# Running products of decays in chunked attention: two scans in place of a tree of products

## The chip, the cores and the metric

The kernel runs on one core of one Trainium2 chip. The metric is the device time of one execution in microseconds (us). Time is told in the profile's names: PE is TensorE (matmuls; PEld its weight loads), DVE is VectorE, ACT is ScalarE, POOL is GpSimd, SP the queue that issues DMAs.

## The reference, cut to what matters

A linear attention with decays, then a mixture of eight experts whose gate weights are balanced by eight Sinkhorn steps, then a wide layer with `h * cos(h)`. Only the attention is touched by the change:

```python
# q, k, v, alpha: (4, 8, 768, 48), alpha in 0.8 .. 1.0
for t in range(S):
    state = alpha[:, :, t, :, None] * state + einsum('bhd,bhe->bhde', k[:, :, t], v[:, :, t])
    y[:, :, t] = einsum('bhd,bhde->bhe', q[:, :, t], state)
x = y as (3072 tokens, 384)
logits = x @ w_gate; P = exp(logits - max); 8 x (rows to sum 1, columns to sum 1, times N/E)
out = sum over e of P[:, e] * (relu(x @ w1[e]) @ w2[e])        # 384 -> 1024 -> 384
h = out @ w_in; result = (h * cos(h)) @ w_out                  # 384 -> 2048 -> 384
```

## The kernel before, in words

**Two stages.** `stage1` interleaves the attention with the first expert's pass; `stage2` runs the other seven experts and the last layer in blocks of 512 tokens. Weights and activations are split into a rounded part and a rest, so that a product takes three matmuls in a fast format.

**Attention.** Tokens are worked in 12 units of 256 (`UNITS`), heads in four pairs, so there are 48 slots (`slots`). A slot's `q`, `k` and decays come in one tile `t` of three rows of 256 (a ring of four tiles, three of which lie in `acc`, whose end is free until the last units' expert products). In a slot the tokens form four chunks of 64, and every chunk two halves of 32. The chunked form needs `q` times the product of decays from the half's start up to its own token, `k` times the product of decays after its token to the half's end, and each half's whole product.

**`ew(i)`** prepares slot `i` with elementwise work. DVE clamps the decays into `a` (`dec`). POOL multiplies `q` by `a`. Then a tree over five levels follows: at level `l` DVE multiplies neighbouring products of decays (128, 64, 32, 16, 8 elements, kept in `pr` at offsets `po[l]`), and half of `q` and half of `k` (256 elements in one view) are multiplied by the products of the level before, at the first level by POOL, at levels 2 to 5 by DVE. One more product of four elements gives the chunks' whole decay, `pr` at `po[6]`. Three products then make `X` (second halves of `q`, once for either head) and `k6` (first halves of `k`), ACT copies the other halves, a reciprocal `rp` of the halves' products is taken, and POOL multiplies parts of `q` and `k` by it in place.

**The main loop** per slot: PE transposes `k6` into bank 0 (`pt`), ACT copies it; PE makes the scores `pg` in bank 1 from `t`; DVE copies them under a mask into `X` (two masked copies); PE makes `k`-`v` products `pk` in bank 2, DVE steps the state four times (`step`); a slot later PE makes the outputs `py` in bank 3, and ACT copies them to `x`. POOL also takes the clamped decays from the given ones and ACT squares and sums the difference into `adev`: if a decay was outside the range, a general path runs instead. `ew(i + 2)` is recorded ahead of slot `i`'s main part.

**What sets the order.** Nothing is issued as it is written: `Plan` records every instruction with its operands, and `issue` then replays a model of the engines with assumed costs (`_cost`) and latencies (`LAT`). It always gives the next instruction to the engine that can start first, by rank (0 first): 0 the attention's main part and Sinkhorn, 1 the experts' matmuls, 2 `ew`, 3 the check of the decays and the decode of the last layer's weights. The device then runs each engine's queue in that fixed order. All planned instructions have one line in the profile (L167), the line that issues them.

**Around it.** A unit's expert block takes its `x`, 8 hidden tiles of 18 matmuls each with 256 columns (banks 4 to 7), ReLU by ACT, and the rest of the rounded hidden layer by DVE (`act_relu`). The gate logits of the units feed `sinkhorn`, which starts when all of them are there; its result goes to DRAM (`pt`) and comes back spread over the partitions (48 transfers). Then the other experts follow.

Of the kernel before, what the change touches and what calls it, by code (L numbers as in the profile page):

```python
# [9 lines left out]
F32 = mybir.dt.float32  # L10
# [5 lines left out]
ALU = mybir.AluOpType  # L16
# [7 lines left out]
E = 8  # L24
# [14 lines left out]
FARENA, RARENA = 9204, 10240  # L39
# [21 lines left out]
class Plan:  # L61
    """Records engine instructions in program order, then issues them in the order in which a model of the
    engines would start them: what feeds the tensor engine first, its own attention products before the experts'."""

    # from one engine's end to another's start, with room for what the model misses
# [44 lines left out]
    def _cost(self, eng, name, aps, kw):  # L110
# [67 lines left out]
class Arena:  # L178
    """Tiles cut out of a buffer, which another stage cuts in another way."""
# [16 lines left out]
    def ring(self, n, shape, dtype):  # L196
        return ring([self.tile(shape, dtype) for i in range(n)])


def ring(tiles):  # L200
    """Tiles that take turns."""
    tiles = itertools.cycle(tiles)
    return lambda: next(tiles)


class Weights:
    """The passes' weights in chunks of 256 hidden units, as rounded parts and their rests."""
# [14 lines left out]
    def prep(self):  # L222
        """Split the next half of a chunk and load another one."""
# [12 lines left out]
class Passes:  # L236
    """Expert passes: hidden layer of a block, then its product with the second weight, LAG tiles behind."""
# [21 lines left out]
    def second(self):  # L259
# [39 lines left out]
class Kernel:  # L299
# [27 lines left out]
    # ------------------------------------------------------------ shared pieces  # L327
# [15 lines left out]
    def gate_weights(self, w):  # L343
        """Gate weights' rounded parts in columns 0..7 and rests in 8..15 of a full stationary tile."""
# [21 lines left out]
    def pieces(self, yt, t0, n):  # L366
        """The last pair's heads, 16 rows to each of the three row tiles."""
# [4 lines left out]
    # ------------------------------------------------------------ attention, chunks of 64  # L372
    def attention(self, pool):
# [6 lines left out]
        prs, k6s = (pool.ring(3, [128, UN], F32) for _ in range(2))  # L380
        rps, kts = pool.ring(3, [128, UN // 32], F32), pool.ring(2, [128, nt0, D], F32)
        yts = pool.ring(1, [128, UN], F32)
        adev, m1, m2 = (pool.tile([128, c], F32) for c in (NPAIR * len(UNITS), 1, 1))
        m2 = m2[0:1]
# [3 lines left out]
        dec, mask = ring([z.tile([128, UN], F32) for z in late]), self.mask  # L388
# [21 lines left out]
        def ew(i):  # L410
            t = loaded.pop(i)
            n = UNITS[slots[i][0]][2]
            X, pr, k6, rp, a = xt(), prs(), k6s(), rps(), dec()
            self.rank(2)
            po, o = {}, 0
            for l in range(1, 7):
                po[l] = o
                o += n >> l
            state[i] = dict(X=X, pr=pr, po=po, k6=k6, qk=t, a=a)
# [16 lines left out]
            tt(V, vw(pr, po[6], [[1, nb]]), vw(pr, po[5], [[2, nb]]), vw(pr, po[5] + 1, [[2, nb]]))  # L436
            for p0, h in ((0, 1), (64, 0)):
                p1 = p0 + 64
                tt(V, vw(X, h * UN + 32, [[64, nb], [1, 32]], p0, p1), vw(t, 32, [[64, nb], [1, 32]], p0, p1), vw(pr, po[5], [[2, nb], [0, 32]], p0, p1))
                A.copy(vw(X, h * UN, [[64, nb], [1, 32]], p0, p1), vw(t, 0, [[64, nb], [1, 32]], p0, p1))  # L440
            tt(V, vw(k6, 0, [[64, nb], [1, 32]]), vw(t, UN, [[64, nb], [1, 32]]), vw(pr, po[5] + 1, [[2, nb], [0, 32]]))
            A.copy(vw(k6, 32, [[64, nb], [1, 32]]), vw(t, UN + 32, [[64, nb], [1, 32]]))
            V.reciprocal(rp[:, :n // 32], vw(pr, po[5], [[1, n // 32]]))
# [17 lines left out]
        V.memset(adev, 0.0)  # L461
        V.tensor_copy(mask, mf)
# [402 lines left out]
```

## Time and profile before

| what | value |
|---|---|
| runs, median of 3 | 2338.79 us (2337.37 to 2341.6) |
| profiled execution, span | 2336.7 us |
| PE busy | 2268.1 us, 97% |
| DVE busy | 1091.0 us, 47% |
| POOL busy | 825.4 us, 35% |
| ACT busy | 782.3 us, 33% |
| chain that ended last | PE 85%, DVE 11% |

The profile gives the span of its execution, from the first to the last instruction, and no other time of it. Times are us, means of one instruction are in ns. [...] A matmul's record can include waiting, so a busy PE is not PE at its peak. The row of a group gives its busy time, the mean of one and the idle time of the engine ahead of it.

### The profile page before, as it was taken

The numbers are of one execution on the slowest core, as the hardware profiler recorded it, in microseconds if no ns is written. First come the engines' busy times: TensorE is split into PE (matmuls) and PEld (weight loads), VectorE is DVE, ScalarE is ACT, GpSimd is POOL, SyncE is SP. The second block draws the span as 40 slices with busy tenths as digits, with TensorE's granted clock in tenths as the row PEclk, the third lists the DMA queues.
The fourth block names the chain that finished last, engine by engine and source line by source line (L and its number), as shares of the span: only waits on it lengthen the run. The fifth ranks groups of instructions, "written<-read, shape, count | busy, mean of one in ns | idle before, by whom it ended". The sixth has DMA issues, their size and how long they took to land.

```text
span 2336.7 us, 32693 instructions
## 1 busy us (share of the span) xinstructions
PE 2268.1 (97%) x12790; PEld 1896.4 (81%) x12790; DVE 1091.0 (47%) x2417; ACT 782.3 (33%) x1628; POOL 825.4 (35%) x716
## 2 busy tenths in 40 slices
PE   4999999988999999999999999999999999999998
PEld 3878888976888888888888888888888888999997
DVE  8989988888422122212221222122222227767665
ACT  3444444221122113112211211211221136666664
POOL 6444443132234115213321422322242245457442
PEclk9988999999999999999999999999999999999999
DMA  4222222344111002001100200110020010000000
GB/s 149 65 66 73 71 73 58 99 119 129 49 30 43 5 10 64 9 6 37 36 7 8 63 10 5 43 30 10 5 63 10 5 43 13 1 8 28 27 28 29
DMA packets 70709, 94.93 MB, mean 41 GB/s; under 512 B 6992, under 2 KB 52624, under 8 KB 70544
## 3 DMA queue, kind: packets, MB, share of 16 engines
q1 hardware_dynamic: 70544, 92.74, 13.8%
q8 instruction: 102, 1.67, 0.3%
q14 instruction: 63, 0.52, 0.1%
HBM read 80.42 MB, written 11.11 MB: 39 GB/s over the span
## 4 chain that ended last, share of the span: by engine, by line
PE 85%; DVE 11%; DMA 1%; issue 1%; POOL 1%; ACT 0%; SPq 0%; DVEq 0%; POOLq 0%; ACTq 0%
PE bank L167 85%; DVE fbuf L167 8%; DVE acc L167 2%; DMA fbuf<-pt 1%; DVE rbuf L167 1%; POOL acc L167 0%; DVE P L167 0%; ACT fbuf L167 0%; POOL fbuf L167 0%; DMA pt<-fbuf 0%; DMA fbuf<-in_w_dram 0%; DMA w<-fbuf 0%; SPq L167 0%; ACT rbuf L167 0%; POOL w31l L167 0%
## 5 line engine op out<-in xcount | busy, mean ns | idle before, releaser
L167 DVE SCALAR_TENSOR_TENSOR rbuf<-bank,rbuf 128x512 fp32r<-128x512 f32 (+1 forms) x432 | 271.8, 629 | 899.8 <-ACT rbuf L167 898.8
L167 ACT ACTIVATE rbuf<-bank 128x512 fp32r<-128x512 f32 (+1 forms) x432 | 237.1, 549 | 964.3 <-PE bank L167 954.5
L167 POOL TENSOR_TENSOR rbuf<-x,rbuf 128x512 fp32r<-128x512 f32 (+1 forms) x162 | 189.6, 1196 | 774.7 <-ACT rbuf L167 738.8
L167 POOL TENSOR_TENSOR acc<-acc,fbuf 128x512 f32<-128x512 f32 (+1 forms) x162 | 183.7, 1161 | 241.1 <-DVE fbuf L167 197.2
L167 PE MATMUL bank<-rbuf,w01h 128*128 128x512 f32 (+1 forms) x648 | 209.2, 379 | 1.3 <-DVE fbuf L167 1.3
L167 PE MATMUL bank<-rbuf,w21h 128*128 128x512 f32 (+1 forms) x648 | 205.7, 374 | 3.5 <-DVE rbuf L167 3.5
L167 PE MATMUL bank<-rbuf,w31h 128*128 128x512 f32 (+1 forms) x648 | 206.5, 376 | 1.9 <-DVE rbuf L167 1.9
L167 PE MATMUL bank<-rbuf,w11h 128*128 128x512 f32 (+1 forms) x648 | 205.2, 374 | 2.2 <-DVE rbuf L167 2.2
L167 POOL TENSOR_TENSOR rbuf<-fbuf,rbuf 128x512 fp32r<-128x512 f32 x96 | 129.0, 1345 | 191.1 <-ACT rbuf L167 190.3
L167 PE MATMUL bank<-rbuf,w20h 128*128 128x512 f32 (+1 forms) x792 | 193.0, 378 | 2.3 <-DVE rbuf L167 2.3
L167 PE MATMUL bank<-rbuf,w00h 128*128 128x512 f32 (+1 forms) x792 | 194.0, 378 | 0.9 <-ACT rbuf L167 0.9
L167 PE MATMUL bank<-rbuf,w10h 128*128 128x512 f32 (+1 forms) x792 | 194.6, 381 | 0.0
L167 PE MATMUL bank<-rbuf,w30h 128*128 128x512 f32 (+1 forms) x792 | 192.8, 378 | 0.0
L167 PEld LDWEIGHTS bank<-rbuf,w20h 128*128 128x128 f32 x792 | 141.8, 190 | 30.0 <-DVE rbuf L167 2.5
L167 PEld LDWEIGHTS bank<-rbuf,w10h 128*128 128x128 f32 x792 | 143.3, 193 | 27.8
L167 PEld LDWEIGHTS bank<-rbuf,w00h 128*128 128x128 f32 x792 | 142.3, 190 | 28.9 <-ACT rbuf L167 1.2
L167 DVE SCALAR_TENSOR_TENSOR fbuf<-fbuf 128x192 uint32<-128x192 uint32 (+2 forms) x288 | 162.5, 565 | 6.1
L167 PEld LDWEIGHTS bank<-rbuf,w30h 128*128 128x128 f32 x792 | 141.9, 190 | 27.8
L167 DVE TENSOR_TENSOR fbuf<-bank,fbuf 128x512 f32<-128x512 f32 x126 | 82.9, 685 | 142.5 <-PE bank L167 138.8
L167 ACT ACTIVATE fbuf<-fbuf 128x512 f32<-128x512 f32 (+1 forms) x204 | 135.0, 662 | 42.4 <-DVE fbuf L167 40.8
L167 DVE TENSOR_SCALAR fbuf<-fbuf 128x192 uint32<-128x192 uint32 (+3 forms) x240 | 102.0, 441 | 99.9 <-ACT fbuf L167 93.5
L167 PEld LDWEIGHTS bank<-rbuf,w01h 128*128 128x128 f32 x648 | 122.4, 194 | 25.9 <-DVE fbuf L167 1.8
(117 smaller groups left out, 4111.5 us busy)
## 6 DMA issues: line engine op xcount, KB each, us to landing
raw<-in_wts_dram SPq DMA_DIRECT2D x64, 384.0 KB, 3.1
acc<-in_qka_dram SPq DMA_DIRECT2D x36, 384.0 KB, 3.2
fbuf<-in_w_dram SPq DMA_DIRECT2D x64, 192.0 KB, 2.4
fbuf<-pt SPq DMA_DIRECT2D x48, 256.0 KB, 4.9
w<-fbuf SPq DMA_DIRECT2D x64, 96.0 KB, 2.4
raw<-w SPq DMA_DIRECT2D x16, 384.0 KB, 3.0
fbuf<-in_vv_dram SPq DMA_DIRECT2D x24, 192.0 KB, 3.2
fbuf<-in_qka_dram SPq DMA_DIRECT2D x12, 384.0 KB, 3.1
```

The costliest lines, as they stand in the source:

```text
L167: getattr(getattr(self.nc, eng), name)(*args, **kw)
```

## The change

In `ew`, the tree is replaced by two scans. A scan goes along a row and keeps `state = data0 * state + data1` at every element. The decays are clamped into a tile `a` of 8 segments of 33 elements, whose first element is zero, and `heads` is one at every segment's first element and zero elsewhere. So each segment restarts at one and then holds the running products of its 32 decays. `f` is the forward scan, `bwd` the same from the end to the start, with views of negative stride. `q` is multiplied by `f` (POOL) and `k` by `bwd` (DVE), each in one product of 256 elements. A half's whole product is the last element of its segment in `f`; `tot` is the product of a chunk's two. POOL's subtraction for the check of the decays moves from the main loop (rank 3) into `ew` (rank 2).

The tiles: `decs` and `fwds` are rings of two of 265 and 264 elements, `bwd` and `heads` are single, `tot` is a ring of three; `k6s` moves into the end of `acc`, where `dec` was. The arena is 28 elements larger; `lt` and `wgs` in `stage1` share a place. `Plan` learns a cost for the scan and the extent of views with negative stride. Comments go too.

```diff
+SEG = 32
+SCAN = (SEG + 1) * (UN // SEG)
...
+        if name == "tensor_tensor_scan":
+            return 67 + 2.1 * n
...
-            V.tensor_scalar(a[:, :n], t[:, 2, :n], AMIN, AMAX, op0=ALU.max, op1=ALU.min)
-            tt(G, t[:, 0, :n], t[:, 0, :n], a[:, :n])
-            tt(V, vw(pr, po[1], [[1, n // 2]]), vw(a, 0, [[2, n // 2]]), vw(a, 1, [[2, n // 2]]))
-            a1 = vw(t, 1, [[UN - 1, 2], [2, n // 2]])
-            tt(G, a1, a1, vw(a, 0, [[1, 2], [2, n // 2]]))
-            for l in range(2, 6):
-                h = 1 << (l - 1)
-                nb = n // (2 * h)
-                tt(V, vw(pr, po[l], [[1, nb]]), vw(pr, po[l - 1], [[2, nb]]), vw(pr, po[l - 1] + 1, [[2, nb]]))
-                a1 = vw(t, h, [[UN - h, 2], [2 * h, nb], [1, h]])
-                tt(V, a1, a1, vw(pr, po[l - 1], [[1, 2], [2, nb], [0, h]]))
-            nb = n // 64
-            tt(V, vw(pr, po[6], [[1, nb]]), vw(pr, po[5], [[2, nb]]), vw(pr, po[5] + 1, [[2, nb]]))
+            V.tensor_scalar(vw(a, 1, seg), vw(t, 2 * UN, flat), AMIN, AMAX, op0=ALU.max, op1=ALU.min)
+
+            V.tensor_tensor_scan(out=f[:, :SCAN], data0=a[:, :SCAN], data1=self.heads, initial=0.0, op0=ALU.mult, op1=ALU.add)
+            V.tensor_tensor_scan(out=vw(bwd, SCAN, [[-1, SCAN]]), data0=vw(a, SCAN, [[-1, SCAN]]), data1=self.heads, initial=0.0, op0=ALU.mult, op1=ALU.add)
+            tt(G, vw(t, 0, flat), vw(t, 0, flat), vw(f, 1, seg))
+            tt(V, vw(t, UN, flat), vw(t, UN, flat), vw(bwd, 2, seg))
+            G.tensor_tensor(out=vw(t, 2 * UN, flat), in0=vw(t, 2 * UN, flat), in1=vw(a, 1, seg), op=ALU.subtract)
+            first, second = SEG, 2 * SEG + 1
+            tt(V, tot[:, :nb], vw(f, first, [[2 * SEG + 2, nb]]), vw(f, second, [[2 * SEG + 2, nb]]))
...
-                G.tensor_tensor(out=d, in0=d, in1=st["a"][:, :n], op=ALU.subtract)
```

**DVE, in the middle of the attention, the work of about one slot.** `bank_97` is a hidden tile of the expert; `fbuf` and `acc` hold the attention's tiles. Before:

```order
L167 TENSOR_TENSOR acc<-acc,fbuf 128x2x16x8
L167 TENSOR_TENSOR fbuf<-acc 128x128
L167 TENSOR_TENSOR acc<-acc,fbuf 128x2x8x16
L167 SCALAR_TENSOR_TENSOR rbuf<-bank_97,rbuf 128x256
L167 TENSOR_TENSOR fbuf<-acc,fbuf 64x4x32 x2
L167 TENSOR_TENSOR fbuf<-acc,fbuf 128x4x32
L167 TENSOR_TENSOR fbuf<-fbuf 128x64
L167 TENSOR_TENSOR fbuf<-fbuf 128x32
L167 TENSOR_TENSOR fbuf<-fbuf 128x16
L167 TENSOR_TENSOR fbuf<-fbuf 128x8
L167 TENSOR_TENSOR fbuf<-fbuf 128x4
L167 RECIPROCAL fbuf<-fbuf 128x8
```
Now (a scan prints as SCALAR_TENSOR_TENSOR of 128x264):

```order
L173 SCALAR_TENSOR_TENSOR rbuf<-bank_97,rbuf 128x256
L173 TENSOR_SCALAR fbuf<-acc 128x8x32
L173 TENSOR_TENSOR fbuf<-acc,fbuf 64x4x32 x2
L173 SCALAR_TENSOR_TENSOR fbuf<-fbuf 128x264
L173 SCALAR_TENSOR_TENSOR fbuf<-fbuf,bank_95 128x48
L173 SCALAR_TENSOR_TENSOR fbuf<-fbuf 128x264
L173 SCALAR_TENSOR_TENSOR fbuf<-fbuf,bank_95 128x48
L173 COPY_PREDICATED fbuf<-mask,bank_94 64x256
L173 SCALAR_TENSOR_TENSOR fbuf<-fbuf,bank_95 128x48
L173 COPY_PREDICATED fbuf<-mask,bank_94 64x256
L173 TENSOR_TENSOR acc<-acc,fbuf 128x256
L173 RECIPROCAL fbuf<-fbuf 128x8
```
The products of 64 to 8 elements and all but one of those of 256 are gone; two scans stand in their place, with the state steps (128x48 from `bank_95`) and masked copies between them.

**POOL, in the attention.** `128x256` on `acc` is a product by decays or the subtraction, `128x2x128` the first level's product, `128x2x4x32` that by `rp`, `rbuf<-x` the rest of an expert's input. Before:

```order
L167 TENSOR_TENSOR acc<-acc,fbuf 128x2x4x32
L167 TENSOR_TENSOR rbuf<-x,rbuf 128x256
L167 TENSOR_TENSOR acc<-acc 128x256
L167 TENSOR_TENSOR acc<-acc,fbuf 128x2x4x32
L167 TENSOR_TENSOR acc<-acc 128x2x128
L167 TENSOR_TENSOR fbuf<-fbuf,acc 128x256
L167 TENSOR_TENSOR acc<-acc 128x256
L167 TENSOR_TENSOR rbuf<-x,rbuf 128x256
L167 TENSOR_TENSOR fbuf<-fbuf,acc 128x2x128
```
Now:

```order
L173 TENSOR_TENSOR acc<-acc,fbuf 128x256 x3
L173 TENSOR_TENSOR acc<-acc,fbuf 128x2x4x32
L173 TENSOR_TENSOR rbuf<-x,rbuf 128x256 x3
L173 TENSOR_TENSOR acc<-acc,fbuf 128x256 x3
L173 TENSOR_TENSOR acc<-acc,fbuf 128x2x4x32
L173 TENSOR_TENSOR fbuf<-fbuf 128x256 x2
L173 TENSOR_TENSOR acc<-acc,fbuf 128x2x4x32
L173 TENSOR_TENSOR acc<-acc,fbuf 128x256 x2
L173 TENSOR_TENSOR fbuf<-fbuf 128x2x4x32
L173 TENSOR_TENSOR acc<-acc,fbuf 128x256
```
The first level's products are gone, and the product by `f` and the subtraction, which both read the slot's scan tiles in `fbuf`, stand together ahead of the product by `rp`.

**PE, the rows up to the expert's first matmul.** `bank_93` holds the transposed `k6`, `bank_94` the scores, `bank_95` the `k`-`v` products, `bank_96` the outputs. Before:

```order
L167 MATMUL bank_93<-ident,fbuf 64x48 x8
L167 MATMUL bank_94<-acc 64x64 x8
L167 MATMUL bank_95<-fbuf 48x48 x8
L167 MATMUL bank_93<-ident,fbuf 64x48 x12
L167 MATMUL bank_94<-acc 64x64 x8
L167 MATMUL bank_96<-fbuf 48x64 x8
L167 MATMUL bank_95<-fbuf 48x48 x8
L167 MATMUL bank_93<-ident,fbuf 64x48 x4
L167 MATMUL bank_94<-acc 64x64 x8
L167 MATMUL bank_96<-fbuf 48x64 x8
L167 MATMUL bank_95<-fbuf 48x48 x8
L167 MATMUL bank_97<-rbuf,w00h 128x256
```
Now:

```order
L173 MATMUL bank_93<-ident,acc 64x48 x8
L173 MATMUL bank_94<-acc 64x64 x9
L173 MATMUL bank_96<-fbuf 48x64 x7
L173 MATMUL bank_95<-fbuf 48x48 x8
L173 MATMUL bank_96<-fbuf 48x64
L173 MATMUL bank_93<-ident,acc 64x48 x8
L173 MATMUL bank_94<-acc 64x64 x8
L173 MATMUL bank_93<-ident,acc 64x48 x8
L173 MATMUL bank_96<-fbuf 48x64 x8
L173 MATMUL bank_95<-fbuf 48x48 x8
L173 MATMUL bank_93<-ident,acc 64x48 x8
L173 MATMUL bank_97<-rbuf,w00h 128x256
```
Transposes now read `acc`, since `k6` lies there, and five slots' transposes (8 each, one row of 8 ahead of this piece) stand ahead of the expert's first matmul, where three slots' did. Further down, 1016 matmuls of 256 columns stood ahead of the attention's last product before, and 883 do now; ahead of the first product of Sinkhorn there are 1475 and 1476.

## Rows read from the trace of the kernel before

**Rows 1.** The page: busy time of each engine, share of the span, instructions.
```profile
PE 2268.1 (97%) x12790; PEld 1896.4 (81%) x12790; DVE 1091.0 (47%) x2417; ACT 782.3 (33%) x1628; POOL 825.4 (35%) x716
```

**Rows 2.** Stages: window, its us, busy per engine (instructions), clock, DMA, GB/s.
```profile
0.00:25.00 25.00, 6.30 (x56) 4.77 (x56) 23.28 (x62) 8.11 (x21) 15.28 (x25) 1.00 0.62 182
25.00:376.80 351.80, 326.48 (x3667) 277.49 (x3668) 316.27 (x985) 167.11 (x550) 167.87 (x225) 0.92 0.24 72
376.80:449.00 72.20, 72.18 (x658) 68.81 (x658) 50.58 (x165) 25.73 (x75) 7.21 (x10) 0.95 0.33 94
449.00:554.00 105.00, 90.03 (x523) 78.33 (x522) 84.32 (x225) 25.78 (x54) 28.47 (x17) 0.95 0.47 116
560.00:1000.00 440.00, 440.00 (x1887) 354.29 (x1886) 128.15 (x239) 95.50 (x160) 128.34 (x94) 1.00 0.12 35
```

**Rows 3.** Pieces of the attention stretch, same view and columns.
```profile
25.00:60.00 35.00, 24.18 (x246) 19.91 (x246) 30.39 (x76) 14.16 (x37) 23.33 (x23) 1.00 0.40 128
154.00:166.00 12.00, 9.89 (x121) 8.62 (x120) 11.81 (x32) 6.36 (x23) 8.82 (x13) 1.00 0.32 100
166.00:181.00 15.00, 14.87 (x120) 11.91 (x122) 8.28 (x33) 4.66 (x18) 1.06 (x2) 0.51 0.12 34
289.00:329.00 40.00, 40.00 (x463) 33.88 (x464) 32.62 (x111) 19.54 (x67) 15.16 (x23) 0.91 0.24 68
329.00:377.00 48.00, 44.26 (x541) 37.14 (x539) 47.12 (x150) 25.55 (x86) 25.53 (x34) 1.00 0.17 52
```

**Rows 4.** The chain of waits from 25 to 376 us, by line.
```profile
by line: PE bank L167 42.4%; DVE fbuf L167 34.5%; DVE acc L167 10.4%; issue 3.5%; DVE rbuf L167 2.6%; POOL acc L167 2.5%; POOL fbuf L167 1.3%; ACT fbuf L167 1.1%; POOL w31l L167 0.5%; ACT rbuf L167 0.4%; ACT w30h L167 0.2%; POOL rbuf L167 0
```

**Rows 5.** Timeline of PE: start, us, what it ran; [idle before <-releaser].
```profile
15.64 0.26 PE L167 MATMUL bank<-ident,fbuf 48*64 48x48 f32 x1 [15.64 <-ACT fbuf L167]
...
358.00 0.88 PE L167 MATMUL bank<-rbuf,w10h 128*128 128x256 f32 x6
358.72 0.51 PE L167 MATMUL bank<-rbuf,w10l 128*128 128x256 f32 x3
```

**Rows 6.** Timeline of DVE where the Sinkhorn chain begins.
```profile
449.43 0.16 DVE L167 TENSOR_SCALAR fbuf<-bank 128x1 f32<-128x1 f32 x1 [0.41 <-PE bank L167]
```

**Rows 7.** DVE, then POOL, by form, 0 to 560 us: xcount | busy, mean ns | idle.
```profile
L167 DVE TENSOR_TENSOR acc<-acc,fbuf 128x256 f32<-128x256 f32 x144 | 71.9, 506 | 0.5
L167 DVE TENSOR_TENSOR fbuf<-fbuf 128x64 f32<-128x64 f32 x48 | 24.8, 521 | 0.2
L167 DVE TENSOR_TENSOR fbuf<-fbuf 128x256 f32<-128x256 f32 x48 | 23.4, 488 | 0.2
L167 DVE TENSOR_TENSOR fbuf<-acc 128x128 f32<-128x128 f32 x48 | 23.1, 486 | 0.3
L167 DVE TENSOR_TENSOR fbuf<-fbuf 128x32 f32<-128x32 f32 x48 | 17.3, 364 | 0.3
L167 DVE TENSOR_TENSOR fbuf<-fbuf 128x16 f32<-128x16 f32 x48 | 16.7, 351 | 0.4
L167 DVE TENSOR_TENSOR fbuf<-fbuf 128x8 f32<-128x8 f32 x48 | 14.2, 298 | 0.5
L167 DVE RECIPROCAL fbuf<-fbuf 128x8 f32<-128x8 f32 x56 | 10.8, 195 | 0.9
L167 DVE RECIPROCAL fbuf<-fbuf 128x24 f32<-128x24 f32 x8 | 2.4, 297 | 0.1
L167 POOL TENSOR_TENSOR acc<-acc 128x256 f32<-128x256 f32 x108 | 88.0, 832 | 58.5 <-PE bank L167 47.6 <-DVE acc L167 8.0 <-issue 2.9
```

**Rows 8.** Timeline of DVE: the product of 64 elements at two places.
```profile
12.96 0.85 DVE L167 TENSOR_TENSOR fbuf<-fbuf 128x64 f32<-128x64 f32 x1
...
309.88 0.22 DVE L167 TENSOR_TENSOR fbuf<-fbuf 128x64 f32<-128x64 f32 x1
```

More of the change, by code (lines that the diff above doesn't have):

```diff
@@ L38 @@
 NRAW = 3
-FARENA, RARENA = 9204, 10240
+FARENA, RARENA = 9232, 10240
+SEG = 32
+SCAN = (SEG + 1) * (UN // SEG)
 DBG = None
@@ L82, in _boxes @@
             p1 = p0 + dims.pop(0)[1]
+        f0 += sum(s * (n - 1) for s, n in dims if s < 0)
+        dims = [[abs(s), n] for s, n in dims]
         if ap.space == PSUM:
@@ L379, in attention @@
         xt = pool.ring(4, [128, 2, UN], F32)
-        prs, k6s = (pool.ring(3, [128, UN], F32) for _ in range(2))
-        rps, kts = pool.ring(3, [128, UN // 32], F32), pool.ring(2, [128, nt0, D], F32)
+        decs, fwds, bwd, self.heads = pool.ring(2, [128, SCAN + 1], F32), pool.ring(2, [128, SCAN], F32), pool.tile([128, SCAN + 1], F32), pool.tile([128, SCAN], F32)
+        rps, tots = pool.ring(2, [128, UN // SEG], F32), pool.ring(3, [128, nt0], F32)
+        kts = pool.ring(2, [128, nt0, D], F32)
         yts = pool.ring(1, [128, UN], F32)
-        adev, m1, m2 = (pool.tile([128, c], F32) for c in (NPAIR * len(UNITS), 1, 1))
-        m2 = m2[0:1]
+        adev = pool.tile([128, NPAIR * len(UNITS)], F32)
+        m1, m2 = tots()[:, 0:1], tots()[0:1, 0:1]
         late = [Arena(self.acc[:, k, NTOK - 4 * UN:]) for k in range(KT)]
         qka = ring([z.tile([128, 3, UN], F32) for z in late + [pool]])
-        dec, mask = ring([z.tile([128, UN], F32) for z in late]), self.mask
+        k6s, mask = ring([z.tile([128, UN], F32) for z in late]), self.mask
         pt0, pk = (self.bank[i][:, :nt0 * D].rearrange("p (t d) -> p t d", d=D) for i in (0, 2))
@@ L412, in ew @@
             n = UNITS[slots[i][0]][2]
-            X, pr, k6, rp, a = xt(), prs(), k6s(), rps(), dec()
+            X, k6, rp, tot, a, f = xt(), k6s(), rps(), tots(), decs(), fwds()
             self.rank(2)
[L415 to L419, printed above, removed]
+            state[i] = dict(X=X, k6=k6, qk=t, tot=tot)
+            nb, seg = n // 64, [[SEG + 1, n // SEG], [1, SEG]]
@@ L437, in ew @@
+            first, second = SEG, 2 * SEG + 1
+            tt(V, tot[:, :nb], vw(f, first, [[2 * SEG + 2, nb]]), vw(f, second, [[2 * SEG + 2, nb]]))
+            tt(V, vw(k6, 0, [[64, nb], [1, 32]]), vw(t, UN, [[64, nb], [1, 32]]), vw(f, second, [[2 * SEG + 2, nb], [0, 32]]))
+            A.copy(vw(k6, 32, [[64, nb], [1, 32]]), vw(t, UN + 32, [[64, nb], [1, 32]]))
+            V.reciprocal(rp[:, :n // SEG], vw(f, first, [[SEG + 1, n // SEG]]))
             for p0, h in ((0, 1), (64, 0)):
                 p1 = p0 + 64
-                tt(V, vw(X, h * UN + 32, [[64, nb], [1, 32]], p0, p1), vw(t, 32, [[64, nb], [1, 32]], p0, p1), vw(pr, po[5], [[2, nb], [0, 32]], p0, p1))
+                tt(V, vw(X, h * UN + 32, [[64, nb], [1, 32]], p0, p1), vw(t, 32, [[64, nb], [1, 32]], p0, p1), vw(f, first, [[2 * SEG + 2, nb], [0, 32]], p0, p1))
@@ L440, in ew @@
                 A.copy(vw(X, h * UN, [[64, nb], [1, 32]], p0, p1), vw(t, 0, [[64, nb], [1, 32]], p0, p1))
-            tt(V, vw(k6, 0, [[64, nb], [1, 32]]), vw(t, UN, [[64, nb], [1, 32]]), vw(pr, po[5] + 1, [[2, nb], [0, 32]]))
-            A.copy(vw(k6, 32, [[64, nb], [1, 32]]), vw(t, UN + 32, [[64, nb], [1, 32]]))
-            V.reciprocal(rp[:, :n // 32], vw(pr, po[5], [[1, n // 32]]))
             a1 = vw(t, 0, [[UN + 32, 2], [64, nb], [1, 32]])
@@ L461, in attention @@
         V.memset(adev, 0.0)
+        for z in (decs, decs):
+            G.memset(z(), 0.0)
+        V.memset(self.heads, 0.0)
+        V.memset(vw(self.heads, 0, [[SEG + 1, UN // SEG]]), 1.0)
         V.tensor_copy(mask, mf)
@@ L475, in attention @@
                 st = state[i]
-                t, k6, X, pr, po = st["qk"], st["k6"], st["X"], st["pr"], st["po"]
+                t, k6, X, tot = st["qk"], st["k6"], st["X"], st["tot"]
                 pt, pg, kt = pt0[:, :nt], pg0[:, :n], kts()[:, :nt]
@@ L504, in step @@
                 def step(j):
-                    V.scalar_tensor_tensor(out=so[:, p, (j + 1) % nt], in0=so[:, p, j], scalar=pr[:, po[6] + j:po[6] + j + 1],
+                    V.scalar_tensor_tensor(out=so[:, p, (j + 1) % nt], in0=so[:, p, j], scalar=tot[:, j:j + 1],
                                            in1=pk[:, j], op0=ALU.mult, op1=ALU.add)
@@ L619, in stage1 @@
         self.wgr = rp.tile([128, KT, 128], F32R)
-        lt, lo, wgs = pool.tile([2 * E, UN], F32), pool.tile([128, UN // 128, E], F32), pool.tile([128, KT, E], F32)
+        lt, lo = pool.tile([128, UN], F32), pool.tile([128, UN // 128, E], F32)
+        wgs, lt = lt[:, 0:KT * E].rearrange("p (k e) -> p k e", k=KT), lt[0:2 * E]
         w = self.wq = Weights(self, 0)
```

1 line of the change is left out of this document (added).

## The prediction

> **What bounds the kernel now.** The page comes first: TensorE is busy 97% of the span [rows 1], which alone would say that nothing on VectorE can matter. The table by stage corrects that [rows 2]. From 25 to 376.8 us, the stretch that holds the attention, VectorE is busy 316 of 352 us; from 376.8 to 449 TensorE is busy all of 72 us with what is left of the first expert; from 449 to 554 the Sinkhorn steps and the gates' transfers run; after that, as from 560 to 1000, TensorE has no gap. So the change can act only before 449, where the chain of Sinkhorn begins at 449.43 [rows 6].
>
> In the attention stretch the chain of waits is shared: TensorE holds 42.4%, VectorE 34.5 + 10.4 + 2.6 = 47.5%, all else some 10% [rows 4]. Busy shares do not show which of the two is slow, since a matmul that waits counts as busy. Rates do [rows 3]. From 329 to 377, a stretch that VectorE holds (47.1 of 48 us busy), TensorE issues 541 matmuls at the full clock: 541/48 = 11.3 per us. From 289 to 329, a stretch that TensorE holds without a gap, it issues 463 in 40 us at a granted clock of 0.91: 463/(40 x 0.91) = 12.7 per us of full clock. In the early 25 to 60 it is 246/35 = 7.0. The whole attention stretch: 3667/(351.8 x 0.92) = 11.3. So TensorE has about 11% to win there, and no more: VectorE is full, but TensorE stands close behind it.
>
> **The change part by part.** *VectorE, removed.* A slot (a pair of heads and a unit of 256 tokens; 48 of them) loses the products of 128, 64, 32, 16 and 8 elements and three of its four products of 256. From [rows 7]: 23.1 + 24.8 + 17.3 + 16.7 + 14.2 = 96.1 us for the five, and 3/4 of 71.9 + 23.4 = 71.5 us for the three; together 167.6 us. The product of four elements stays as `tot`. That the product of 64 elements takes longer in the mean (521 ns) than that of 128 (486 ns) shows where much of this goes: the same 64 elements took 0.22 us once and 0.85 us another time [rows 8]. Such an instruction stands still inside; the likely reason is POOL, which works on the same slot's data at that time. Eight instructions go and two come, so there are fewer places to stand still.
>
> *VectorE, added.* Two scans of 264 elements per slot, 96 in all. No row shows a scan. The nearest is the product of 256 elements with two operands, 506 ns in the mean, which for 264 makes 0.52 us: the lower end, no gain below it being likely since a scan also reads two operands and writes one. The upper end is the costliest row per element, the reciprocal: (297 - 195)/(24 - 8) = 6.4 ns an element, so 195 + 256 x 6.4 = 1.83 us. I take 0.80 us, nearer to the product, since a scan is one multiply and one add for each element and divides nothing, but above it, since each element needs the one before. That makes 96 x 0.80 = 77 us (50 to 176). Net VectorE loses 167.6 - 77 = 91 us, with ends of 118 less and 8 more.
>
> [...]
>
> *Where that time was.* About 45.5 of the 48 slots fall into 25 to 376.8, so VectorE's load there goes from 316 to 316 - 91 x 45.5/48 = 230 us. In a stretch of some 316 us that is 73%. From 289 to 329, where TensorE held the chain, VectorE was busy 32.6 of 40, 82% [rows 3]. So what is late next is TensorE, and the stretch can be no faster than TensorE's own rate. At 12.7 per us the 3667 matmuls need 3667/12.7 = 288 us of full clock against 351.8 x 0.92 = 324 now: **35 us less**. I leave the 28 us that the half clock costs there (0.08 x 351.8) as they are.
>
> *The order on TensorE.* The planner issues by its own costs, so the whole order is new. Counted over it, 1016 matmuls of the first expert (256 columns, gate weights among them) stood ahead of the attention's last product, and 883 do now; ahead of Sinkhorn's first it is 1475 and 1476. So 133 matmuls move behind the attention. One costs (358.72 - 358.00)/6 = 0.12 us [rows 5], in all 16 us. The 35 us hold for an unchanged set of matmuls: what leaves the stretch is paid in the next one, where TensorE is full, so the move itself costs nothing and wins nothing up to 449.
>
> *POOL.* Per slot it loses one product of 256 elements (the first level's, 832 ns in the mean [rows 7]): 40 us in all, on an engine that is busy 168 of 352 us [rows 2]. It hides behind VectorE and TensorE; nothing is booked. Its subtraction of the clamped decays moves from the main loop into the slot's preparation, ahead of the last product by `rp` that releases TensorE's scores. If that were not covered by the two slots of lead, it would cost up to 48 x 0.83 = 40 us.
>
> *The added wait.* The `X` products on VectorE now read a `q` that POOL has multiplied by the forward scan just issued. In the order, the backward scan, the product of `k` and some two more instructions stand between: 0.8 + 0.5 us at the least, against 0.83 us for POOL. Queued behind it are the next slot's clamp, the masked copies from PSUM and the rests of the hidden layer, for which TensorE's banks wait. I cost it at nothing; before, the product of the second level waited for POOL in the same way. The rings of two for `decs` and `fwds` come round two slots later, long after POOL's last read; nothing.
>
> *Start and the rest.* TensorE's first product comes at 15.64 us [rows 5], after two slots' preparation on VectorE, which is busy 23.3 of the first 25 us [rows 2]. Two slots at 91/48 = 1.9 us less would make 3.8; the memsets of the scan's tiles take some of it: **3 us**. DMAs are the same in number and size; the planner puts the loads earlier with the slots. From 449 on the same products, transfers and decode stand in the order; its decode moves partly ahead of Sinkhorn, where VectorE has room (50.6 of 72.2 us busy [rows 2]). Nothing is booked there.
>
> **The sum.** The profiled execution has a span of 2336.7 us; the median of the runs, 2338.8, lies 2.1 above, which I take as what surrounds a span. 2336.7 - 35 - 3 = 2298.7, and with 2.1, 2300.8: **2301 us**.
>
> **The rivals.** *The clock comes back* (chance 0.13). [...]
>
> *TensorE's fixed order keeps half of the waits* (0.17). Scores, masked copies and state steps still alternate between TensorE and VectorE, and POOL, ScalarE and issue hold a tenth of the chain [rows 4]. If only half of 38 us is won: 2320.
>
> *The change moves nothing* (0.09). The attention gets shorter by just the 133 matmuls that left it, 16 us, and pays them back before Sinkhorn, whose place in TensorE's order is the same: 2339. For it speaks that TensorE is 97% busy; against it, the 11.3 against 12.7.
>
> *The scan costs as much as the reciprocal* (0.08), which ends slower. At 1.83 us VectorE carries (8 x 45.5/48 = 8 us) more, the attention takes 351.8 x 324/316 = 361 us, and the 133 matmuls come on top: 2339 + 9 + 16 = 2364. The loss begins where the attention shrinks by less than 16 us, that is at a VectorE load of 316 x 336/352 = 302, or a scan of about 1.6 us; the forecast is untouched up to about 1.1 us, where VectorE reaches the 82% of the stretch from 289.
>
> **How the numbers follow.** The forecast itself has 0.53, and by its own steps reaches from 2288 to 2316. The range takes in the clock rival below and nearly all of the half-won case above, and leaves out no change and slower (0.17): 2270 to 2334. About 0.2% (4.7 us) is what a measurement can tell from no change. Faster by more: 0.53 + 0.13 + 0.17 = 0.83; the same: 0.09; slower: 0.08.
>
> **What would show it.** Right: scans of 0.6 to 1.1 us; VectorE busy about 230 us over the attention; the last masked copy some 50 us earlier; then about 88 instead of 72 us of TensorE without a gap; Sinkhorn's first scalar step near 411; from there to the end 1887 us as now. Wrong: a scan above 1.6 us; VectorE still some 90% busy; a rate of TensorE in the attention that stays at 11.3 with VectorE at 73%, which would mean that the waits are in the fixed order; or POOL named as what VectorE's `X` products wait for.

## The result

The changed kernel takes 2269.89 us (median of 4 runs, 2266.45 to 2275.03) against 2338.08 of before in the same comparison: a ratio of 0.9721 [0.9698, 0.9743], 68 us less. The forecast was 2301, that is 38 us less. The time lies at the lower end of the range (2270), and the gain is nearly double the one forecast, not because one term was too small: about 30 us come from a stretch of the program in which the prediction had booked nothing.

First the page of the kernel after: busy time and share of the span. It answers to [rows 1].

```profile
span 2269.0 us, 32397 instructions
PE 2228.4 (98%) x12790; PEld 1885.1 (83%) x12790; DVE 1024.1 (45%) x2131; ACT 782.4 (34%) x1628; POOL 798.5 (35%) x670
```

The same 12790 matmuls cost TensorE 40 us less busy time. The change takes no work from TensorE, so this line is where the surprise begins.

The scans, by form, from 0 to 560 us of the kernel after (count | busy us, mean ns | idle before):

```profile
L173 DVE TENSOR_TENSOR_SCAN fbuf<-fbuf 128x264 f32<-128x264 f32 x96 | 79.9, 842 | 1.3
```

The first product in PE's timeline of after, against 15.64 in [rows 5]:

```profile
8.20 1.11 PE L173 MATMUL bank<-ident,acc 48*64 48x48 f32 x5 [8.20 <-ACT acc L173]
```

Where the Sinkhorn chain begins, DVE's timeline of after, against 449.43 in [rows 6]:

```profile
413.28 0.15 DVE L173 TENSOR_SCALAR fbuf<-bank 128x1 f32<-128x1 f32 x1
```

So up to Sinkhorn 36 us are won, where the forecast had 38 (start near 411). From there to the end it was 2336.7 - 449.43 = 1887.3 us and now is 2269.0 - 413.28 = 1855.7: another 32 us, unforecast.

The stretches of after, with the columns of [rows 2]: window, its us, busy per engine (instructions), clock, DMA, GB/s.

```profile
8.20:413.28 405.08, 395.04 (x4386) 341.57 (x4387) 328.33 (x947) 198.02 (x642) 157.12 (x198) 0.97 0.30 91
25.00:60.00 35.00, 28.57 (x277) 23.24 (x274) 28.57 (x65) 19.14 (x58) 20.13 (x22) 1.00 0.43 137
60.00:331.00 271.00, 271.00 (x3254) 227.94 (x3256) 223.08 (x652) 142.63 (x480) 115.63 (x154) 0.96 0.25 76
250.00:300.00 50.00, 50.00 (x611) 41.69 (x609) 39.28 (x118) 27.52 (x92) 20.85 (x30) 0.97 0.29 85
1000.00:1500.00 500.00, 500.00 (x2186) 410.27 (x2185) 110.62 (x166) 115.21 (x191) 159.39 (x115) 1.00 0.09 27
```

The same view of the kernel before, in the stretch from its first product to Sinkhorn and in two others:

```profile
15.64:449.43 433.79, 405.39 (x4384) 351.44 (x4384) 376.16 (x1169) 197.67 (x638) 180.31 (x239) 0.93 0.26 76
60.00:331.00 271.00, 260.23 (x2907) 222.46 (x2908) 240.89 (x769) 129.25 (x433) 120.19 (x171) 0.90 0.23 69
1000.00:1500.00 500.00, 500.00 (x2144) 402.60 (x2143) 109.18 (x164) 108.42 (x182) 146.39 (x108) 1.00 0.08 22
```

Read the last row of each. From 1000 to 1500 TensorE is busy all 500 us at the full clock in both, and yet issues 2186 matmuls of 512 columns instead of 2144: one every 228.7 ns instead of every 233.2. Starts in the trace say it more exactly: over 5700 matmuls of the expert passes 228.9 ns against 233.3. With 7 passes of 864 such matmuls that is 6048 x 4.4 ns = 27 us, in a part of the program whose matmuls the change left alone. "PE busy without a gap" is no lower limit.

Then the attention. From 60 to 331 us TensorE has no gap left (271.00 of 271), and the chain of waits of after, from 25 to 331, by line, is TensorE's where it was shared in [rows 4]:

```profile
by line: PE bank L173 91.0%; DVE fbuf L173 5.0%; DVE acc L173 1.1%; issue 0.3%; DVE rbuf L173 0.1%
```

A measure helps from here on. Each run lists its span and its mean granted clock. Span x clock is the **full-clock time**: what the run would take at a granted clock of 1.00 throughout (the clock is told as a share of the full one), if all of it followed TensorE's clock; the rest of the span is put down to the stretches at half of that (0.51 from 166 to 181 us in [rows 3]). Not all of it does follow, so the rest is an upper bound: the slowest and the fastest run of e2 differ by 30 us in it and by 21 us in time. A split into full clock and half clock is therefore good to some us. Beside the median the table gives means over the runs of each kernel (three to eight; 8 for before, from the first comparison), and the interval of the 512-column matmuls in the expert passes. The last column is explained with the experiments.

| kernel | median us | full clock | half clock costs | interval, ns | tokens - weights, bytes mod 256 |
|---|---|---|---|---|---|
| before | 2336.6 | 2297 | 37 | 233.3 | 224 |
| e1_arena | 2308.6 | 2270 | 37 | 228.9 | 64 |
| e10_before_rbuf_first | 2297.4 | 2255 | 41 | 226.7 | 0 |
| after | 2269.9 | 2251 | 18 | 228.9 | 64 |
| e2_after_shift | 2303.7 | 2273 | 28 | 233.3 | 32 |
| e4_rbuf_first | 2261.7 | 2238 | 21 | 226.7 | 0 |
| e5_rbuf_4096 | 2295.6 | 2275 | 20 | 232.4 | 128 |
| e8_all_512 | 2259.1 | 2239 | 19 | 226.7 | 0 |
| e3_scan_twice | 2317.5 | 2266 | 51 | 228.9 | 64 |
| e6_forward_twice | 2278.4 | 2249 | 27 | 228.9 | 64 |
| e7_no_backward | 2275.2 | 2244 | 30 | 228.9 | 64 |

### The profile page after: what moved, and what is told of

Its sections match the earlier page's. It is cut to its first block, busy times and chain, and to the rows that moved or that the text cites. A ratio compares the mean times of both kernels' runs of the same rounds, so it can differ in the third digit from the quotient of the medians.

```text
span 2269.0 us, 32397 instructions
## 1 busy us (share of the span) xinstructions
PE 2228.4 (98%) x12790; PEld 1885.1 (83%) x12790; DVE 1024.1 (45%) x2131; ACT 782.4 (34%) x1628; POOL 798.5 (35%) x670
## 4 chain that ended last, share of the span: by engine, by line
PE 93%; DVE 4%; DMA 1%; issue 0%; ACT 0%; DVEq 0%
PE bank L173 93%; DVE fbuf L173 3%; DMA fbuf<-pt 1%; DVE acc L173 0%; DVE P L173 0%; DVE rbuf L173 0%; DMA w<-fbuf 0%; DMA fbuf<-in_w_dram 0%; DVE x L173 0%; ACT fbuf L173 0%; ACT rbuf L173 0%; DVEq L813 0%; DVEq L173 0%
## 5 line engine op out<-in xcount | busy, mean ns | idle before, releaser
L173 POOL TENSOR_TENSOR acc<-acc,fbuf 128x512 f32<-128x512 f32 (+1 forms) x234 | 247.3, 1079 | 262.9 <-DVE fbuf L173 227.9
L173 PE MATMUL bank<-rbuf,w01h 128*128 128x512 f32 (+1 forms) x648 | 202.4, 370 | 0.2 <-DVE fbuf L173 0.2
L173 PE MATMUL bank<-rbuf,w31h 128*128 128x512 f32 (+1 forms) x648 | 201.1, 369 | 0.1
L173 DVE SCALAR_TENSOR_TENSOR fbuf<-fbuf 128x192 uint32<-128x192 uint32 (+2 forms) x288 | 168.2, 585 | 5.9
L173 DVE TENSOR_SCALAR fbuf<-fbuf 128x192 uint32<-128x192 uint32 (+4 forms) x252 | 99.7, 410 | 100.1 <-ACT fbuf L173 91.0
L173 PEld LDWEIGHTS bank<-rbuf,w21h 128*128 128x128 f32 x648 | 119.2, 189 | 26.9 <-DVE rbuf L173 5.7
```

The source lines that it names most:

```text
L173: getattr(getattr(self.nc, eng), name)(*args, **kw)
```

## Experiments on the unforecast 30 us: where the tokens lie

The diff makes the buffer `fbuf` 28 elements longer. Behind it lies `rbuf`, from which every expert matmul reads its moving operand; its address went from 114272 to 114368 (96 bytes and not 112: the addresses told here are all multiples of 32). The weights (`w`, the stationary operand in the expert passes) begin at 16512 in both.

**The arena alone.**

```diff
 (kernel before)
-FARENA, RARENA = 9204, 10240
+FARENA, RARENA = 9232, 10240
```

> The kernel before with one number changed: the buffer of attention tiles is 9232 elements long instead of 9204, as in the changed kernel, so that the buffer behind it, from which every expert matmul reads its tokens or its hidden layer, begins 96 bytes further on, at a multiple of 64 bytes (114368) instead of an odd multiple of 32 (114272). The order on every engine is the same as before. Question: why does a 512-column matmul take 228.9 ns from start to start after about 505 us in the changed kernel and 233.3 before, which is some 28 of the 68 us won and is no work of the attention. Theory of the address: the new place alone does it; interval 228.9 ns, about 6000 matmuls x 4.4 ns = 26 us and a little from the last layer, time 2308 to 2314. Rival, the order or the instructions around the matmuls do it: interval 233.3, time 2338 (2333 to 2342).

Measured: 2308.58 us, a ratio to before of 0.9872 [0.9842, 0.9901], 28 us less, with every engine's order that of before. The 512-column interval is 228.9 ns, and from 1000 to 1500 us stand 2186 matmuls, the count of after:

```profile
1000.00:1500.00 500.00, 500.00 (x2186) 410.90 (x2185) 110.61 (x166) 115.58 (x193) 156.90 (x115) 1.00 0.09 25
```

The rival is out: nothing of the scans or of the planner's order is needed for this part of the gain. Sinkhorn starts at 447.80 in this run, so from there to the end it takes 2308.7 - 447.80 = 1860.9 us, 26 less than before. The changed kernel takes 1855.7: of its 32 us behind Sinkhorn the place gives 26, and some 5 come with its other order; where they arise was not followed.

**The change, with the buffer put back.**

```diff
 (kernel after)
-FARENA, RARENA = 9232, 10240
+FARENA, RARENA = 9224, 10240
...
-        lt, lo = pool.tile([128, UN], F32), pool.tile([128, UN // 128, E], F32)
+        lt, lo = pool.tile([128, UN], F32), self.P[:, 0:UN // 128]
```

> The changed kernel with that buffer moved back to an odd multiple of 32 bytes (114336): the arena has 9224 elements, and the small tile of gate sums that stood at its end lies in the place of the gate weights. Theory of the address: interval of the 512-column matmuls 233.3 ns as before, time 2270 + 28 = 2298 (2294 to 2302), while Sinkhorn still starts near 413 us. Rival, the order or the instructions do it: interval 228.9, time 2270.

Measured: 2303.66 us (2292.35 to 2313.07), 0.9835 [0.9791, 0.988], interval 233.3; in the same stretch the count of before:

```profile
1000.00:1500.00 500.00, 500.00 (x2144) 402.37 (x2143) 107.88 (x162) 112.39 (x187) 154.31 (x113) 1.00 0.09 25
```

This is what the scans give without the other place, and it lies within 3 us of the forecast of 2301. The time is 1.7 us above the expected range, and the other expectation, Sinkhorn near 413 us, failed in the profiled run: it starts at 429.69. TensorE's order up to there is that of after, instruction by instruction; the difference is the clock, 0.92 against 0.97:

```profile
8.20:429.69 421.49, 411.46 (x4387) 355.49 (x4388) 328.20 (x947) 197.49 (x642) 155.63 (x198) 0.92 0.29 87
```

**Buffers exchanged.**

```diff
 (kernel after)
-        self.fbuf = const.tile([128, FARENA], F32, name="fbuf")
         self.rbuf = const.tile([128, RARENA], F32R, name="rbuf")
+        self.fbuf = const.tile([128, FARENA], F32, name="fbuf")
```

> The changed kernel with the two buffers in the other order: the one that TensorE reads begins at 77440, a multiple of 128 bytes (now an odd multiple of 64), the one of the attention's tiles behind it at 118400. Same order of instructions. If the address matters only within 64 bytes: interval 228.9, time 2270. If within 128 bytes too: an interval below 228.9, and 26 us less for every 4.4 ns, 2245 or so. If the address has no part in it: 2270.

Measured: 2261.69 us, 0.9664 [0.9634, 0.9695]; interval 226.7, 2208 matmuls in that stretch:

```profile
1000.00:1500.00 500.00, 500.00 (x2208) 414.36 (x2207) 113.40 (x171) 115.64 (x192) 162.37 (x119) 1.00 0.10 28
```

The place still had something to give, and at that point "the coarser the alignment, the better" looked like the rule.

**Alignment or distance.** Two runs set these apart. In the first the tokens go 384 bytes further, to a multiple of 4096, and the weights stay; in the second weights and tokens both begin at multiples of 512.

```diff
 (e4_rbuf_first; lo and adev lie in P, FARENA = 9184)
+        self.pad = const.tile([128, 32], F32, name="pad")
+        self.mask = const.tile([128, UN], U8, name="mask")
         self.rbuf = const.tile([128, RARENA], F32R, name="rbuf")
...
 (for e8_all_512 pad and mask stand ahead of self.w instead, Lg and P behind rbuf)
```

> The run with the two buffers exchanged, whose matmuls of 512 columns came every 226.7 ns (228.9 in the changed kernel, 233.3 before), with the buffer that TensorE reads 384 bytes further on, at 77824, a multiple of 4096 bytes instead of 128; the weights stay where they are. Two small tiles (gate sums, the sums of the check) lie in the place of the gate weights to make room, and the buffer of the attention's tiles is shorter. If coarser alignment goes on paying: interval under 225 and time 2250 or less. If 128 bytes are the end of it: interval 226.7, time 2262. If it is the distance to the weights' addresses and not the alignment (there 77440 and the weights' 16512 left the same rest by 512, here they do not): an interval that rises again to 228.9 or more, 2275 to 2290.

> As the run with the buffer at a multiple of 4096, but the weights too are moved, so that both the weights and the buffer that TensorE reads begin at multiples of 512 bytes (16896 and 76288). If the weights' own alignment matters (they begin at a multiple of 128 in all other runs): an interval below that of the other runs. If only the moving operand's matters: the interval of the run at 4096. If only the distance between the two matters: 226.7 ns, that of the exchange, since both have the same rest by 512 again; 2262.

Measured: 2295.57 us (0.9833 [0.9807, 0.9858]), interval 232.4, for the buffer at a multiple of 4096; 2259.1 us (0.9678 [0.9651, 0.9704]), interval 226.7, with the weights moved too. So alignment is the wrong idea: the best-aligned buffer is among the slow ones. What the two fast layouts (e4 and e8) share is the difference of the two addresses, a multiple of 512 bytes. Neither address decides by itself: beyond a multiple of 256, tokens and weights lie at 128 and 128 in e4, at 0 and 128 in e5, at 0 and 0 in e8, and only e5 is slow. (With the weights move the raw weights and two constant tiles, which no matmul of these passes reads.) The stretch from 1000 to 1500 us (columns of [rows 2]), first of e5, then of e8:

```profile
1000.00:1500.00 500.00, 500.00 (x2153) 405.41 (x2153) 109.15 (x164) 113.55 (x189) 157.82 (x114) 1.00 0.10 27
```

```profile
1000.00:1500.00 500.00, 500.00 (x2207) 414.15 (x2207) 113.68 (x171) 115.07 (x191) 161.48 (x117) 1.00 0.10 28
```

**A sweep in one run.**

```diff
 (e4_rbuf_first, stage2)
+SHIFT = 0, 32, 64, 96, 128, 160, 192, 224, 256, 288, 320, 384, 448, 480
...
+                if p < E and t0 % (NTOK // 2) == 0:
+                    ra = Arena(self.rbuf)
+                    ra.o = SHIFT[2 * (p - 1) + t0 // (NTOK // 2)] // 4
+                    xhl = ring([[ra.tile([128, KT, BLK], F32R) for _ in range(2)] for _ in range(2)])
+                    hh, hl = (ra.ring(LAG + 1, [128, BLK], F32R) for _ in range(2))
...
```

> The run with the two buffers exchanged, in which the seven expert passes after the first use fourteen places for the tokens and the hidden layer, three blocks each: 0, 32, 64, 96, 128, 160, 192, 224, 256, 288, 320, 384, 448 and 480 bytes further on (for 16 ring slots fewer are needed there, so there is room). The distance from the weights to the tokens is then that many bytes beyond a multiple of 512. If the distance by 512 decides, the interval of the 512-column matmuls in the steady part of each piece is 226.7 ns at 0, 228.9 at 64, 233.3 at 32 and 480, 232.4 at 384, as in the runs so far, and the other places show whether any is below 226.7. If it was the whole layout or the order and not the distance, the interval stays 226.7 in all pieces. Time 2275 to 2290, for most places are slower than the first.

Where one place follows another, the first tokens of the new one overwrite some columns of hidden tiles that are still to be read, so this kernel's values differ there. Measured: 2294.77 us, more than expected, as more of the places are slow than I had assumed. Pieces of 60 us each, at shifts of 64, 128, 256, 320 and 384 bytes:

```profile
700.00:760.00 60.00, 60.00 (x263) 49.21 (x262) 13.79 (x21) 10.74 (x19) 13.35 (x11) 1.00 0.04 9
...
900.00:960.00 60.00, 60.00 (x258) 48.25 (x257) 13.97 (x21) 10.95 (x20) 13.54 (x11) 1.00 0.03 9
...
1300.00:1360.00 60.00, 60.00 (x267) 49.67 (x266) 13.43 (x21) 12.06 (x21) 13.96 (x11) 1.00 0.04 9
...
1500.00:1560.00 60.00, 60.00 (x264) 49.25 (x263) 13.85 (x21) 12.06 (x21) 13.96 (x11) 1.00 0.04 9
1600.00:1660.00 60.00, 60.00 (x260) 48.66 (x259) 13.68 (x21) 14.79 (x25) 19.44 (x14) 1.00 0.10 29
```

Mean distance from start to start over the steady part of each piece, some 330 matmuls:

| shift, bytes | 0 | 32 | 64 | 96 | 128 | 160 | 192 | 224 |
|---|---|---|---|---|---|---|---|---|
| ns | 226.9 | 233.3 | 228.9 | 233.3 | 233.3 | 234.3 | 233.3 | 233.3 |
| shift + 256: ns | 226.7 | 233.3 | 228.9 | not tried | 232.4 | not tried | 233.3 | 233.3 |

The expectations on the known places hold, and the period is shorter than I had put it: 256 bytes, not 512 (only 128 and 384 differ, by 0.9 ns). Two of the eight places are good, 0 and 64; six are much alike. Before the change the distance stood at 224, and the 28 elements moved it to 64. Of the places tried, 0 is the best.

**The exchange on the kernel before.** The same exchange of two lines as above, in the kernel before.

> The kernel before with nothing changed but the order of the two buffers: the one that TensorE reads at 77440, as in the exchange on the changed kernel. Every engine's order is that of before. If distance and attention are separate causes that add: at full clock 2297 - 5700 x 6.6 ns (233.3 to 226.7) = 2259 and a little for the rest, with the 37 us of half clock of before 2295; the changed kernel with the exchange (2262) then is 33 us faster, which is what the scans are worth at equal places. If the change of the attention is worth less at this place, 2270 to 2285.

Measured: 2297.44 us, 0.9838 [0.9803, 0.9874]; interval 226.7, full-clock time 2255 (2259 expected). In the stretch from 1000 to 1500 us stands the count of the other two kernels at distance 0:

```profile
1000.00:1500.00 500.00, 500.00 (x2207) 414.03 (x2206) 113.60 (x171) 115.67 (x192) 161.29 (x117) 1.00 0.09 28
```

Within some us the two causes add. It also gives the worth of the scans, with the order that came with them, at three equal or equally slow places:

| distance | without scans | with scans | scans |
|---|---|---|---|
| 224 and 32 (both 233.3 ns) | before 2336.6 | e2 2303.7 | -33 us |
| 64 | e1 2308.6 | after 2269.9 | -39 us |
| 0 | e10 2297.4 | e4 2261.7 | -36 us |

Exchanging two lines of allocation was worth 41 us on the kernel before, as much as the whole change of the attention.

## Experiments on the attention

**Both scans twice.**

```diff
-            V.tensor_tensor_scan(out=f[:, :SCAN], ...)
-            V.tensor_tensor_scan(out=vw(bwd, SCAN, [[-1, SCAN]]), ...)
+            for _ in range(2):
+                V.tensor_tensor_scan(out=f[:, :SCAN], ...)
+                V.tensor_tensor_scan(out=vw(bwd, SCAN, [[-1, SCAN]]), ...)
```

> The changed kernel with both scans issued twice (the same result again), 96 scans of 842 ns more, 81 us on VectorE; the planner counts half for each, so that its model of VectorE stays the same. Theory that VectorE had been the bound and is now hidden with some 18% of slack: from 25 to 331.5 us it was busy 251.8 of 306.5; with 43 slots x 1.68 = 72 us more it carries 324 and the attention stretches to 324/0.9 = 360 us, as long as before, so Sinkhorn starts 40 to 55 us later and the time is 2310 to 2325; a second scan costs far more than nothing because the slack is used up. Rival, TensorE alone sets the attention now and VectorE runs beside it whatever it costs: 2270 to 2278. The clock: if gaps on TensorE bring the half clock, the mean granted clock up to Sinkhorn falls from 0.97 towards the 0.93 of before.

Measured: 2317.52 us, 0.9923 [0.9886, 0.9961]; 48 us above the changed kernel, so VectorE's slack is used up, and 9 above e1, which has the tree of products at the same place: with 192 scans of 789 ns, in effect 1.58 us for each of 96, the change would be worth less than nothing. The expected slowing of VectorE is the smaller part, though: 15 us at full clock, 33 from the half clock. Sinkhorn starts at 465.35, 52 us later, as expected, but the granted clock up to there is 0.89 and not between 0.97 and 0.93. The scans, and the stretch from 60 to 331 us:

```profile
L173 DVE TENSOR_TENSOR_SCAN fbuf<-fbuf 128x264 f32<-128x264 f32 x192 | 146.2, 789 | 1.5
60.00:331.00 271.00, 257.71 (x2734) 215.36 (x2734) 236.62 (x623) 123.25 (x418) 105.33 (x139) 0.82 0.23 69
```

**The forward scan twice,** the planner's cost for it halved:

```diff
+            for _ in range(2):
+                V.tensor_tensor_scan(out=f[:, :SCAN], ...)
```

> The changed kernel with the forward scan alone issued twice: 48 scans of 0.84 us more, as if either scan took 1.26 us. Both scans twice gave 2317.5, of which 15 us at full clock (span times granted clock: 2251 to 2266) and 33 us from more time at half clock. Theory of the slack, as forecast (untouched up to scans of 1.1 us, a loss from 1.6 on): at full clock 0 to 8 us more, time 2270 to 2290 depending on the clock. Rival, VectorE is a bound already in the changed kernel and every microsecond on it shows: half of what both scans cost, 2290 to 2298.

Measured: 2278.42 us, 0.9745 [0.972, 0.9769]. At full clock 2249 against 2251: 40 us more on VectorE cost nothing there. The 8 us in the median are half clock (27 against 18).

```profile
60.00:331.00 271.00, 268.45 (x3162) 225.93 (x3158) 244.26 (x680) 142.17 (x481) 117.75 (x156) 0.92 0.26 77
```

**No backward scan.**

```diff
-            V.tensor_tensor_scan(out=vw(bwd, SCAN, [[-1, SCAN]]), ...)
-            tt(V, vw(t, UN, flat), vw(t, UN, flat), vw(bwd, 2, seg))
+            tt(V, vw(t, UN, flat), vw(t, UN, flat), vw(f, 1, seg))
```

> The changed kernel without the backward scan: k is multiplied by the forward products (which leaves out that part of the computation). VectorE loses 48 x 0.84 = 40 us of its 328 up to Sinkhorn. Theory that TensorE alone sets the stretch from 60 to 331 us, where its records leave no gap: at full clock the same but for 2 us at the start, 2247 to 2252, time 2260 to 2275 by the clock. Rival, waits for VectorE hide inside TensorE's records there: 10 us or more less at full clock, time 2255 or less.

Measured: 2275.15 us, 0.9733 [0.9709, 0.9757]; no gain in time, and 7 us less at full clock, between what the two theories said (up to 4, or 10 and more).

```profile
60.00:331.00 271.00, 269.94 (x3225) 226.59 (x3225) 196.78 (x614) 143.48 (x484) 106.80 (x155) 0.93 0.26 76
```

Matmuls per us of full clock in the three: 2734/(271 x 0.82) = 12.3, 12.7 and 12.8; after 3254/(271 x 0.96) = 12.5, before 2907/(271 x 0.90) = 11.9. Between 197 and 244 us of VectorE in this stretch TensorE's own rate hardly moves. VectorE is at most a weak bound of the changed kernel: taking 40 us more from it wins 7 us at full clock and nothing clear in time. One reservation holds for these three runs: the planner ordered anew in each. Ahead of the attention's last product stand 883 matmuls of 256 columns in after and in e6 (whose order differs elsewhere), 860 in e3 and 808 in e7, so part of their differences, the 7 us of e7 above all, can be the order. Nor does a run separate the scans from the order that came with them, from `k6` being made earlier in the slot, or from POOL's subtraction moving there; the 33 to 39 us are the worth of all of it.

What stays open is the half clock. It goes with gaps on TensorE only in part: from 60 to 331 us the run with most gaps (e3, 257.71 of 271 us busy) has most of it (0.82), but e7 has nearly none (269.94 of 271) and 0.93. In e2, whose order is that of after but for the place of one small tile, one stretch shows it plainly:

```profile
250.00:300.00 50.00, 50.00 (x470) 41.43 (x468) 30.74 (x96) 20.81 (x70) 14.71 (x22) 0.69 0.20 63
```

TensorE was busy all of 50 us and was granted 0.69; in after the same stretch has 0.97. The four runs of e2 lie between 0.982 and 0.995 over the span, and their times between 2292 and 2313 us, 21 us apart for one program. What brought the half clock there, no run here shows.

## Why the prediction was right, and where only its sum was

**Right: what bounds the kernel.** TensorE, hidden behind VectorE, was late next; VectorE's load fell to 223.08 of 271 us, 82%. That is more than the 73% forecast, but it is the share up to which the prediction held VectorE harmless, and e6 bears that out at full clock.

**Right: the scan.** 842 ns in the mean against 800 taken; 79.9 us in all against 77. Part of the mean goes with POOL: the 26 scans during which no POOL instruction ran took 683 to 710 ns, the other 70 took 893 in the mean. The same split bears out what the prediction took as the likely reason for the uneven product of 64 elements: in the trace of before, the 14 that met no POOL instruction took 211 to 224 ns, the other 34 took 647 in the mean.

The rival of the costly scan fell. Its point of decision, about 1.6 us, came true by luck: at 1.58 us in effect, e3 is 9 us slower than the tree at the same place (e1), but by the half clock (51 against 37), which the prediction left as it was; at full clock it is 4 us faster.

**Mis-sized: what VectorE loses.** 91 us were booked; by the page its busy time falls from 1091.0 to 1024.1, by 67. Added up one by one, its records come to 1196.6 us before and 1110.1 now, 87 less. So the rows of the groups were right, but they count the time in which one record overlaps the next on the same engine, and the 316 us from which the prediction took them count it once. Hence 28.57 + 223.08 = 252 us from 25 to 331 and not 230. It did no harm, as TensorE's stretch set the end.

**Right: the move of 133 expert matmuls, POOL and the added wait cost nothing** that shows: no gap on TensorE from 60 us on, and Sinkhorn's start at 413 against 411. The closeness of the two is luck of that run, since e2, with the same order on TensorE, has 429.69.

**Too small: the start.** The first product comes 7.4 us earlier, not 3. The estimate took VectorE's 1.9 us per slot and two slots of preparation. In the trace of after the first product starts when only the first slot is prepared (its scans run from 5.19 to 6.94 us, the second slot's start at 8.42 and 10.91); in the diff, the `k6` that it reads is made ahead of `X`, where it came last before.

**Wrong inside, right in sum: the 35 us of TensorE's rate.** The step divided all 3667 matmuls of 25 to 376.8 by 12.7 per us of full clock. The rate did come about (12.5 from 60 on), but the gain did not. From first product to Sinkhorn, at full clock: 433.79 x 0.93 = 403 us before, 405.08 x 0.97 = 393 after. So about 10 us were won where 35 stood. Up to the attention's last product (at 392.0 us before, at 339.7 now) it is 346 against 320 us of full clock, but 16 of these 26 us are paid back behind it, where 57 us become 74, as the prediction said of the 133 matmuls that moved there. Two things took the rest. The step also applied the rate to the start-up from 25 to 60, where 277 matmuls in 35 us, 7.9 per us, came out against 7.0: at 12.7 the 246 of before would take 19 us, at 7.9 they take 31, and that is 12 of the missing 25. And the 12.5 belongs to a lighter mix: 25% of the matmuls from 60 to 331 have 256 columns, where 28% had. By the rate of the tail, 475 in 57.4 us, an estimate is that the mix alone lifts the 11.9 of before to 12.2. That the mix accounts for all the rest is not shown.

**Wrong: "I leave the 28 us that the half clock costs there as they are".** In the same stretch they went from 433.79 x 0.07 = 30 to 405.08 x 0.03 = 12 us. By the means of all runs, 37 against 18 to 28 for the orders with scans (after, e2, e4, e5, e8). The rival in which the clock comes back had a chance of 0.13; what sets the granted clock, no run shows. In this pair of profiles the clock is half of the gain up to Sinkhorn; at equal places, by the means of the table, it is 9 to 20 of the scans' 33 to 39 us. Start 7, rate 10 and clock 18 make 35: the forecast's 38 came out by two errors that cancel, which is luck.

**Wrong: "Nothing is booked there", after 449.** This is the step behind the other 30 us. The diff had said that the arena is 28 elements larger; the prediction treated that as bookkeeping, since no instruction changed, and counted 1887 us from Sinkhorn to the end. Measured 1856; e1 shows that 26 of the 32 us come from the place alone. The profile of before could not have shown the cause, as it holds one layout only. What it did show is a steady interval of 233 ns (440 us for 1887 matmuls in the last row of [rows 2]), and the prediction took it as given.

## What to carry to other kernels

An edit that resizes a buffer moves every buffer behind it (here `rbuf`, by 96 bytes): compare the addresses of what TensorE reads before and after, and when a time changes in a stretch whose instructions did not, compare the start-to-start interval of like matmuls there. Where matmuls run back to back, try the distance between weights and moving operand (here a multiple of 256 bytes, 233.3 to 226.7 ns, some 40 us of 2340) before touching any work. And keep rate and granted clock as separate terms of a sum, in the start-up stretch apart from the rest, or two wrong terms will pass for a right one. Nor subtract sums of an engine's rows from the busy time of a stretch, when the records of that engine overlap.

The fastest kernels of this study are the changed kernel with the two buffers exchanged or with weights and tokens both at multiples of 512: 2261.69 and 2259.1 us, 0.9664 [0.9634, 0.9695] and 0.9678 [0.9651, 0.9704] of before.

## What was unexpected of the hardware

- With TensorE busy without a gap at the full clock and a weight load for every matmul, a 512-column matmul started every 226.7 to 226.9 ns (e4, e8, e10 and the sweep e9), 228.9 (after, e1, e9) or 232.4 to 234.3 (before, e2, e5, e9), by the distance between the two operands' addresses in a partition, with a period of 256 bytes but for 0.9 ns over the places tried. The alignment of either address by itself does not decide (226.7 in e4, 232.4 in e5, 226.7 in e8). What in the hardware makes the distance count, no run here shows.
- The half clock came in a stretch in which TensorE's records leave no gap at all (50.00 of 50 us at 0.69), and the four runs of that program differ by 21 us.
- A scan of 264 elements on VectorE took 683 to 710 ns where no POOL instruction ran beside it (26 of 96), and 893 ns in the mean where one did; a product of 64 elements 211 to 224 ns and 647 ns (before).
